# Decode attention beside an MLP on one core: from two-head to four-head groups, with hand-written waits

## The chip, the cores and the metric

The kernel runs on one core of one Trainium2 chip. A core has five engines that run their own instruction streams: TensorE (PE, matrix products into PSUM), VectorE (DVE), ScalarE (ACT), GpSimd (POOL) and SyncE (SP, which here only issues transfers). Sixteen DMA engines, called lanes below, move data between the chip's main memory (HBM) and the core's SBUF; SBUF and PSUM have 128 partitions. The metric is the device time of one execution in microseconds, lower is better; the median of the runs is given.

## The reference: what is computed

Four tokens (B = 4, one position each, D = 512) go through one block that adds two branches:

```
xn  = layernorm(x)
A   = attention(xn): q = xn @ wq, 32 heads of 128
      scores = q . k_cache * 128**-0.5        k_cache: [4, 32, 4096, 128]
      p = softmax(scores); o = p @ v_cache    v_cache: [4, 32, 4096, 128]
      return o @ wo
B   = mlp-mixer(xn): the shifts move along a sequence of length 1, so h @ w2 gets zeros
      x1 = xn;  return x1 + gelu(layernorm(x1) @ w3) @ w4
out = x + A + B
```

All data are 32-bit floats. The caches are 268 MB each and every byte of them is used once: 128 pairs of batch and head, each with 4096 keys and 4096 values of 128 elements. wq and wo are 8.4 MB each, w3 and w4 3.7 MB each. In all 561 MB are read.

## The kernel before

**Tiling.** Two heads are one pair, and there are 64 pairs. The keys of a pair are one contiguous stretch of 4 MiB. Partition p gets 64 consecutive rows of 128 elements, so one transfer is 128 rows of 32 KiB, eight for each lane, and partitions 0 to 63 hold the first head, 64 to 127 the second. Values lie in the same way. SBUF has six slots of 32 KiB a partition (`SLOTS = 6`), and keys, values and weights rotate through them.

**The loop over pairs** (`for i in range(NP + 1)`, L313) issues the transfers of the keys and values of pair i+1, works on the keys of pair i and finishes pair i-1:

- `products` (L205) multiplies the keys in place by the query on VectorE. The query has been spread to all partitions by a TensorE product (`queries`, L200) for four pairs at once and is read from PSUM. It is issued in two pieces of 2048 and 6144 elements.
- `row_sums` (L209) adds up each row of 128 products: 64 scores a partition.
- `max_begin` (L214, L216) takes each partition's maximum and turns the column of maxima into a row with a TensorE product; `weights` (L222 to L234) takes each head's maximum over that row, spreads its negative with another TensorE product, and has ScalarE compute exp(score - maximum) and its sums into `pw`.
- `values` (L244) contracts `pw` with the values: 16 TensorE products a pair (two records in the trace for each, 32-bit), four column groups side by side, into `PVS`.
- Every fourth pair `outputs` (L251 to L262) gathers and divides by the sums; every sixteenth `spread` (L265 to L268) writes a token's result to `X`.

**Around the loop.** `layernorm`, `transposed` and the query projection (L188) run while the first keys arrive. The MLP's upper half (L277 to L289) runs beside the first keys, its lower half (L307) near the end. wo arrives last in five pieces of falling size (`wo_load`, L346) and is multiplied by `X` in the same order (L358, L364, L369); the result is copied (L372) and stored (L374).

**What sets the order.** The source order above is each engine's order. The Tile framework puts the waits between the engines and between a buffer's last reader and its next transfer. All big transfers are issued from SP, in source order, in one queue; SP stops at a transfer whose slot is still in use. The loops are unrolled.

## Time and profile before

| what | us |
|---|---|
| median of 3 runs | 1317.51 |
| lowest and highest run | 1314.52, 1317.52 |
| span of the profiled execution, first to last instruction | 1312.6 |
| VectorE busy | 1161.9 (89%) |
| TensorE busy | 522.8 (40%) |
| ScalarE busy | 82.6 (6%) |
| all 16 lanes together, share of the span on the big queue | 99.4% |

The page gives the profiled execution its span, 1312.6 us, and no other time; the runs are 1.9 to 4.9 us above that span. The page's second part shows the span in 40 slices: one digit a slice is a busy share in tenths. The lines by engine name source line, engine, operation and tile, then how often they occur, the busy time in us and the mean of one in ns. A window row gives, for a stretch of the span, each engine's busy time with the number of instructions, the clock granted to TensorE as a share of full speed, the lanes' busy share and the GB/s they moved. In the timeline the first number of a row is the start in us, the second the duration.

### The profile page before, as it was taken

What the parts mean: (1) busy time and instruction counts of PE and PEld (TensorE: products, weight loads), DVE (VectorE), ACT (ScalarE), POOL (GpSimd) and SP (SyncE); (2) the same over time, 40 slices, a digit from 0 to 9 for tenths busy, and PEclk for the clock granted to TensorE, in tenths of its full rate; (3) what the DMA queues carried; (4) which work ended last, traced back from release to release, by engine and by line L of the source; (5) the groups of instructions that cost most, each with busy time, mean ns of one, the idle gap of its engine ahead of it and who ended that gap; (6) DMA issues with size and microseconds to landing.
All of it is one profiled execution on the core that took longest, in us unless ns stands there. A gap on an engine that the chain in (4) does not pass through costs nothing.

```text
span 1312.6 us, 6935 instructions
## 1 busy us (share of the span) xinstructions
PE 522.8 (40%) x2736; PEld 169.0 (13%) x2736; DVE 1161.9 (89%) x386; ACT 82.6 (6%) x349; POOL 15.4 (1%) x77
## 2 busy tenths in 40 slices
PE   5415334434424424434433433433443342443345
PEld 1101101111111101111110110111111110111111
DVE  2798999999999999989989999999999999999992
ACT  0100000000000000000000000000000000000000
POOL 0000000000000000000000000000000000000000
PEclk9666577566566666656656756756665756666768
DMA  9999999999999999999999999999999999999997
GB/s 404 434 432 430 431 430 432 431 431 432 433 431 431 430 432 430 430 432 432 432 431 431 432 431 431 431 431 432 432 431 431 432 431 431 431 431 431 433 431 314
DMA packets 19928, 561.46 MB, mean 428 GB/s; under 512 B 2220, under 2 KB 2228, under 8 KB 2488
## 3 DMA queue, kind: packets, MB, share of 16 engines
q1 hardware_dynamic: 19880, 561.00, 99.4%
q8 instruction: 22, 0.36, 0.1%
q14 instruction: 10, 0.08, 0.0%
q10 hardware_dynamic: 16, 0.01, 0.0%
HBM read 561.00 MB, written 0.01 MB: 427 GB/s over the span
## 4 chain that ended last, share of the span: by engine, by line
DMA 58%; DVE 33%; PE 6%; issue 2%; ACT 0%; SPq 0%; DVEq 0%
DMA k<-in_A_k_cache_dram 55%; DVE sc L209 19%; DVE k L205 13%; PE pv L244 4%; DMA wo<-in_A_wo_dram 3%; PE oz L254 1%; PE pm L216 0%; ACT os L251 0%; PE pn L224 0%; DVE gm L222 0%; DVE rm L214 0%; PE oz L257 0%; PE total L364 0%; PE total L369 0%; SPq L88 0%
## 5 line engine op out<-in xcount | busy, mean ns | idle before, releaser
L205 DVE TENSOR_TENSOR k<-k,qb 128x2048 f32<-128x2048 f32 (+1 forms) x128 | 560.0, 4415 | 58.1 <-DMA k<-in_A_k_cache_dram 57.9
L209 DVE TENSOR_REDUCE sc<-k 128x64 f32<-128x8192 f32 x64 | 555.5, 8679 | 4.9
L244 PE MATMUL pv<-v,pw 128*32 128x512 f32 x2048 | 371.2, 891 | 81.0 <-issue 79.8
L216 PE MATMUL pm<-ident,rm 128*1 128x128 f32 x128 | 37.4, 395 | 590.0 <-DVE rm L214 590.0
L244 PEld LDWEIGHTS pv<-v,pw 128*32 128x32 f32 x2048 | 92.9, 156 | 304.0 <-issue 302.7
L216 PEld LDWEIGHTS pm<-ident,rm 128*1 128x1 f32 x128 | 7.1, 80 | 635.8 <-issue 626.5
L226 ACT COPY nm<-pn 128x2 f32<-128x2 f32 x64 | 10.2, 160 | 1027.4 <-PE pn L224 1027.4
L222 DVE TENSOR_REDUCE gm<-pm 1x2 f32<-1x128 f32 x64 | 17.9, 279 | 50.0 <-PE pm L216 50.0
L224 PE MATMUL pn<-gm,ones 1*128 1x2 f32 x128 | 37.1, 357 | 24.3 <-DVE gm L222 24.3
L234 ACT ACTIVATE pw<-sc,nm 64x64 f32<-64x64 f32 x128 | 44.5, 347 | 6.0
L224 PEld LDWEIGHTS pn<-gm,ones 1*128 1x128 f32 x128 | 31.7, 305 | 56.2 <-DVE gm L222 53.4
L200 PE MATMUL qb<-q_sb,selb 64*128 64x512 f32 x32 | 19.9, 703 | 24.7 <-DVE k L205 24.0
L230 POOL MEMSET pw<- 128x128 f32 x64 | 13.0, 204 | 1229.9 <-PE pv L244 1229.9
L234 ACT ACTIVATION_READ_ACCUMULATOR pw<-sc,nm 64x1 f32 x128 | 23.6, 185 | 0.0
L254 PE MATMUL oz<-sel,os 128*128 128x8 f32 x128 | 16.9, 259 | 11.2 <-ACT os L251 11.2
L254 PEld LDWEIGHTS oz<-sel,os 128*128 128x128 f32 x128 | 15.5, 191 | 26.5 <-ACT os L251 26.5
L259 DVE RECIPROCAL rz<-oz 128x8 f32<-128x8 f32 x16 | 3.3, 205 | 15.3 <-PE oz L257 15.2
L214 DVE TENSOR_REDUCE rm<-sc 128x1 f32<-128x64 f32 x64 | 14.1, 220 | 1.7
L251 ACT COPY os<-pv 128x512 f32<-128x512 f32 x16 | 9.4, 585 | 94.8 <-PE pv L244 94.8
L267 PE MATMUL xt<-sel,lt 128*128 128x32 f32 x8 | 2.2, 365 | 29.3 <-DVE lt L265 29.3
L188 PE MATMUL pq<-wq,X 128*32 128x512 f32 x64 | 10.1, 792 | 9.2 <-DMA wq<-in_A_wq_dram 9.2
L372 DVE COPY q_sb<-total 64x256 f32<-64x256 f32 x1 | 0.4, 416 | 11.5 <-PE total L369 11.5
(77 smaller groups left out, 80.7 us busy)
## 6 DMA issues: line engine op xcount, KB each, us to landing
k<-in_A_k_cache_dram SPq DMA_DIRECT2D x64, 4096.0 KB, 40.7
v<-in_A_v_cache_dram SPq DMA_DIRECT2D x64, 4096.0 KB, 41.6
wq<-in_A_wq_dram SPq DMA_DIRECT2D x2, 4096.0 KB, 16.8
wo<-in_A_wo_dram SPq DMA_DIRECT2D x1, 4096.0 KB, 40.9
w<-in_B_w_dram SPq DMA_DIRECT2D x2, 1792.0 KB, 23.3
w<-in_B_w_dram SPq DMA_DIRECT2D x1, 3584.0 KB
wo<-in_A_wo_dram SPq DMA_DIRECT2D x1, 2048.0 KB, 35.9
wo<-in_A_wo_dram SPq DMA_DIRECT2D x1, 1024.0 KB
```

The source lines that it names most:

```text
L200: nc.tensor.matmul(QBC[z], selb[HALF * u:HALF * (u + 1), b], q_sb[HALF * u:HALF * (u + 1), n, :], start=True, stop=True)
L205: nc.vector.tensor_tensor(out=K[i][:, c0:c1, :], in0=K[i][:, c0:c1, :], in1=q, op=ALU.mult)
L209: nc.vector.reduce_sum(sc, K[i], axis=AX.X)
L214: nc.vector.reduce_max(rm, SC[i], axis=AX.X)
L216: nc.tensor.matmul(pm, rm, ident, start=True, stop=True)
L222: nc.vector.tensor_reduce(gm, ROWMAX[i].rearrange("o (e p) -> o e p", e=2), axis=AX.X, op=ALU.max, negate=True)
L224: nc.tensor.matmul(pn, ones[0:1, :], gm, start=True, stop=True)
L226: nc.scalar.copy(nm, pn)
L230: nc.gpsimd.memset(pw[:, :, 8 * r2:8 * r2 + 8], 0.0)
L234: nc.scalar.activation(o, sc[s, :].rearrange("p (g w) -> p g w", w=4), AF.Exp, bias=nm[s, e:e + 1], scale=1.0, accum_out=rs[s, r, e:e + 1])
L244: nc.tensor.matmul(pv[32 * t:32 * t + 32, :], pw[:, g, :], V[i][:, 4 * g:4 * g + 4, :], start=(r == 0 and g < 4), stop=(r == QUAD - 1 and ...
L254: nc.tensor.matmul(oz[:, 0, :], os[:, m, :], sel.rearrange("p (r m e) -> p m r e", m=4, e=2)[:, m], start=(m == 0), stop=(m == 3))
```

## The change

The whole kernel body is written anew; the sums it computes stay.

- Four heads are one group, 32 groups. One transfer is 8 MiB: 128 rows of 64 KiB. Partition p holds 128 rows of 128 elements, 32 partitions a head.
- SBUF holds three slots of 64 KiB a partition: keys rotate through two (S0, S1), values use one (S2). wq uses S2 first, w3 and w4 use S1, the small tensors of the start lie in S0. The last group's values go to S0 in three pieces, wo in five pieces to S2.
- The order of transfers on SP is wq (2), w3, w4, K0, K1, V0, K2, V1, K3 and so on. K0 waits for the queries (`d_Q`), K1 for the lower half of the MLP (`p_dn`), which now runs at the start; K(g+2) waits for the row sums of group g (`k_free`), V(g+1) for the contraction of group g (`v_free`).
- Each query is spread by VectorE: a copy that repeats its elements, then a transpose in blocks of 32 by 32 (`qx`, `qb`). Products and row sums are one instruction each, over 16384 elements, both inputs in SBUF. `contract` issues 32 TensorE products of 512 columns a group, `weights` four exponentials of 32 partitions each. The maxima are taken with a copy, a transpose and a reduction on VectorE. The TensorE products for spreading (L200, L224) and for turning maxima (L216) are gone, and POOL's clearing of `pw` (L230) too.
- The waits are written by hand. `own` makes VectorE wait for its own instruction; `take` is an instruction of its own that waits for a semaphore and takes the count back.
- The loops over groups are hardware loops (`Fori`) on TensorE, ScalarE and VectorE (two groups a turn on VectorE). SP's stream stays unrolled.
- The result is stored in four quarters instead of two halves.

The core of the diff, with the new stretches that the prediction speaks of:

```diff
-    R = 2 * S // P
-    NP = B * H // 2
-    kv = ctx.enter_context(tc.tile_pool(name="kv", bufs=SLOTS))
+    HG = 4
+    NG = B * H // HG
+    C = HG * S // P
+    G4 = C // 4
+    ROW = C * DH
+    slots = [sbuf(f"slot{i}", [P, ROW]) for i in range(3)]
...
+    def take(e, s, n=1):
+        e.wait_ge(s, n).then_inc(s, -n)
+    LAST = ((0, C // 2), (C // 2, 3 * C // 4), (3 * C // 4, C))
...
+        @block.sync
+        def _(e):
+            def load_k(g):
+                e.dma_start(KS[g % 2][:, :], group(kf, g)).then_inc(s_k[g % 2], 16)
...
+            e.wait_ge(d_Q, 1)
+            load_k(0)
+            e.wait_ge(p_dn, 1)
+            load_k(1)
+            for g in range(NG - 1):
+                if g > 0:
+                    take(e, v_free)
+                e.dma_start(S2[:, :], group(vf, g)).then_inc(s_v, 16)
+                if g + 2 < NG:
+                    take(e, k_free[g % 2])
+                    load_k(g + 2)
+            take(e, k_free[0])
...
+            take(e, v_free)
+            for n, (c0, c1) in enumerate(PIECES):
+                e.dma_start(wo_sb[:, c0:c1, :], wo_r[:, c0:c1, :]).then_inc(s_wo[n], 16)
...
+            with nc.Fori(0, NG - 1, 1, engines=[ET.PE]):
+                take(e, s_v, 16)
+                take(e, a_w)
+                contract(V3).then_inc(p_pv, 1)
+                outputs(v_free)
...
+            with nc.Fori(0, NG - 1, 1, engines=[ET.Activation]) as g:
+                weights()
+                e.drain().then_inc(a_sc, 1)
+                outputs(OS[:, bass.ds(g, 1), :])
...
+            with nc.Fori(0, NG, 2, engines=[ET.DVE]) as g:
+                for n in range(2):
+                    K = KS[n][:, :].rearrange("p (c d) -> p c d", c=C)
+                    own(e.tensor_copy(qx[:, :].rearrange("p (h r) -> p h r", h=4),
+                                      Q[:, bass.ds(g + n, 1), :].rearrange("p o h -> p (o h)").unsqueeze(2)
+                                      .to_broadcast([P, 4, 32])))
+                    own(e.transpose(qb[:, :], qx[:, :]))
+                    take(e, s_k[n], 16)
+                    own(e.tensor_tensor(out=K, in0=K, in1=qb[:, :].unsqueeze(1).to_broadcast([P, C, DH]), op=ALU.mult))
+                    take(e, a_sc)
+                    e.reduce_sum(sc[:, :], K, axis=AX.X).then_inc(d_self, 1)
+                    e.wait_ge(d_self, 1).then_inc(k_free[n], 1)
+                    own(e.reduce_max(st[:, 0:1], sc[:, :], axis=AX.X), 2)
+                    own(e.tensor_copy(mx[:, :], st[:, 0:1].to_broadcast([P, 32])))
+                    own(e.transpose(mt[:, :], mx[:, :]))
+                    e.tensor_reduce(st[:, 1:2], mt[:, :], axis=AX.X, op=ALU.max, negate=True).then_inc(d_m, 1)
```

In the new tail, chunks 0 to 23 of wo go to `y`, chunks 24 to 31 to `total` in four column groups of 128 columns each (two groups of 256 before).

## The prediction

> **What bounds the kernel now.** The first page is read from the top: busy shares, then the slices, then the queues.

> ```profile
> PE 522.8 (40%) x2736; PEld 169.0 (13%) x2736; DVE 1161.9 (89%) x386; ACT 82.6 (6%) x349; POOL 15.4 (1%) x77
> DMA  9999999999999999999999999999999999999997
> GB/s 404 434 432 430 431 430 432 431 431 432 433 431 431 430 432 430 430 432 432 432 431 431 432 431 431 431 431 432 432 431 431 432 431 431 431 431 431 433 431 314
> q1 hardware_dynamic: 19880, 561.00, 99.4%
> DMA k<-in_A_k_cache_dram 55%; DVE sc L209 19%; DVE k L205 13%; PE pv L244 4%; DMA wo<-in_A_wo_dram 3%; PE oz L254 1%; PE pm L216 0%; ACT os L251 0%; PE pn L224 0%; DVE gm L222 0%; DVE rm L214 0%; PE oz L257 0%; PE total L364 0%; PE total L369 0%; SPq L88 0%
> ```

> The lanes are busy in every slice but the last, at a steady 431 GB/s, and the big queue alone fills 99.4% of all lanes. VectorE is second with 89%. The chain of waits names VectorE for a third of the span, but that is an echo: it follows the keys' transfer back to the instruction that freed its slot, while the lanes went on with earlier transfers. 561.00 MB at 431 GB/s are 1301.6 us of the 1312.6 us span; 11 us are start and end. So the change can win only by moving the same bytes faster or by trimming the two ends, and it loses as soon as lanes run dry.

> ```profile
> SPq L95 <- DVE rm L214: 618.7, 60, 15.2
> SPq L99 <- PE pv L244: 516.6, 60, 9.8
> DVE k L205 <- DMA k<-in_A_k_cache_dram: 57.9, 53, 23.6
> ```

> These are the waits. SP waits for slots nearly all the time (618.7 and 516.6 us), yet the lanes don't idle, because transfers are queued ahead. VectorE waits for keys only 57.9 us in all, 23.6 of them for the first: it has little slack.

> **What one packet costs.** The queue view for two stretches, a steady one (100 to 1250 us) and the end, where wo's small pieces arrive (1300 to 1308 us): first all packets, then the big queue's packets, MB and share of 16 lanes.

> ```profile
> DMA packets 17039, 495.91 MB, mean 431 GB/s; under 512 B 1889, under 2 KB 1889, under 8 KB 1889
> q1 hardware_dynamic: 17011, 495.53, 100.2%
> DMA packets 389, 1.85 MB, mean 231 GB/s; under 512 B 53, under 2 KB 53, under 8 KB 296
> q1 hardware_dynamic: 388, 1.83, 55.6%
> q8 instruction: 1, 0.02, 0.9%
> ```

> The packets under 512 B are the transfers' completions; I charge them to the data. Steady: 17011 - 1889 = 15122 packets of 32 KiB took 100.2% x 16 x 1150 us = 18437 us, 1219 ns each. End: 388 - 53 = 335 packets of 5463 B on average took 55.6% x 16 x 8 us = 71.2 us, 212 ns each. The line through both is 0.0369 ns a byte plus 11 ns a packet. Keys and values are 16384 packets before and 8448 after (63 transfers of 128 and the last values in three pieces): 7936 x 11 ns / 16 lanes = **5.5 us less**. Bounds: nothing if a 64 KiB row costs what two of 32 KiB do (no row shows so large a packet), 6.4 us if the fixed part is 13 ns. I take the line. [...]

> **VectorE for four heads.** Groups by form, busy us and mean ns of one:

> ```profile
> L209 DVE TENSOR_REDUCE sc<-k 128x64 f32<-128x8192 f32 x64 | 555.5, 8679 | 4.9
> L205 DVE TENSOR_TENSOR k<-k,qb 128x6144 f32<-128x6144 f32 x64 | 418.9, 6545 | 0.0
> L205 DVE TENSOR_TENSOR k<-k,qb 128x2048 f32<-128x2048 f32 x64 | 146.2, 2285 | 58.1 <-DMA k<-in_A_k_cache_dram 57.9
> L222 DVE TENSOR_REDUCE gm<-pm 1x2 f32<-1x128 f32 x64 | 17.9, 279 | 50.0 <-PE pm L216 50.0
> L214 DVE TENSOR_REDUCE rm<-sc 128x1 f32<-128x64 f32 x64 | 14.1, 220 | 1.7
> L288 DVE STREAM_TRANSPOSE w<-w 128x448 f32<-128x448 f32 x1 | 0.6, 645 | 0.0
> L289 DVE COPY gT<-w 128x56 f32<-128x56 f32 x1 | 0.2, 191 | 0.0
> ```

> Before, two pairs cost 2 x (8.679 + 6.545 + 2.285 + 0.279 + 0.220) = 36.0 us. The two products give 1.04 ns an element plus 155 ns, the two reductions L209 and L214 the same slope. So 16384 elements cost 17.19 and 17.20 us. The small ones, moved along that slope: copies of 128 and 32 elements 0.27 and 0.17 us (from L289), transposes of 128 and 32 0.31 and 0.21 (from L288), reductions of 128 and 32 0.29 and 0.19 (from L214). Sum 35.8 us: larger instructions save what the transposes cost. On top come ten `take` and `own` waits and half a loop turn. A wait that is an instruction of its own stands before L234 on ScalarE:

> ```profile
> 1249.78 0.16 ACT L226 COPY nm<-pn 128x2 f32<-128x2 f32 x1 [18.30 <-PE pn L224]
> 1250.02 0.35 ACT L234 ACTIVATE pw<-sc,nm 64x64 f32<-64x64 f32 x1
> 1251.01 6.27 PE L244 MATMUL pv<-v,pw 128*32 128x512 f32 x32 [1.27 <-issue]
> ```

> The gap there is 0.08 us; I take 0.1 us a wait and 0.3 us for the loop, T = **37.1 us** a group. The lanes need 16.78 MB / 431 GB/s = 38.9 us, less 0.18 for the packets: 38.7. VectorE stays hidden, with 1.6 us to spare a group (38.9 - 36.0 = 2.9 before). The dropped TensorE, ScalarE and POOL steps (L200, L216, L224, L226, L230) lay beside the lanes and are worth nothing; so do the larger exponentials.

> **Do three slots keep the lanes fed?** Take group g in the steady state, its keys' last byte at 0. V(g-1), K(g+1), V(g) follow, 19.4 us each. K(g+2) must be issued before V(g) ends at 58; it waits for row sums that end near 35. V(g+1) must be issued before K(g+2) ends, 19.4 us after V(g) landed; it waits for one contraction of 32 products. A pair's 16 take 6.27 us in the row above, so 12.5 us, and everything queued behind that `take` on SP is one transfer. Adding 1 us from issue to first byte, some 5 us are left. Cost nothing; without that cover, each us over costs 30 us.

> The tightest point is the start:

> ```profile
> 0.74 0.38 SPq L103 DMA_DIRECT2D w<-in_B_w_dram  x1
> 27.77 5.20 PE L188 MATMUL pq<-wq,X 128*32 128x512 f32 x32 [4.78 <-DMA wq<-in_A_wq_dram]
> 32.19 0.60 ACT L191 ACTIVATE q_sb<-pq 128x512 f32<-128x512 f32 x1 [21.13 <-PE pq L188]
> 37.53 8.75 DVE L205 TENSOR_TENSOR k<-k,qb 128x2048 f32<-128x2048 f32 x2 [23.57 <-DMA k<-in_A_k_cache_dram]
> ```

> wq's second half was there at 27.8 behind 1.8 MB of w3, which now come later: 23.5. Product 5.2, scaling twice 0.6, transpose of 1024 elements 1.2 and a copy 0.3: K0 is issued near 31, while w3 and w4 keep the lanes busy until 40. K1 waits for the MLP's lower half and must be queued before K0 ends at 59.5: that leaves w3's reader 28 us from w3's landing near 32 for a dozen short steps (L288 and L289 above are two) and 60 records of products at the rate of L188, some 15 us in all. VectorE starts K0 at 60, its row sums end at 60 + 34.4 + 0.3 = 94.7, and K2 must be issued before V0 ends at 98: 3 us to spare, less on lanes that run ahead. I take 0; bounds 0 and +2. Each later group gains 1.6 us of slack. The start has two more branch and semaphore steps on SP ahead of its first transfer (at 0.74 above): +0.4, bounds 0 and +1.

> **The end.** Lanes, and the chain of the last pair:

> ```profile
> 1300.00:1302.00 2.00, 2.00 (x24) 0.45 (x19) 0.00 (x0) 0.00 (x0) 0.00 (x0) 1.00 0.94 389
> 1302.00:1304.00 2.00, 1.49 (x16) 0.22 (x12) 0.00 (x0) 0.00 (x0) 0.00 (x0) 1.00 0.70 289
> 1304.00:1306.00 2.00, 1.45 (x16) 0.30 (x10) 0.00 (x0) 0.58 (x1) 0.00 (x0) 1.00 0.50 203
> 1306.00:1308.00 2.00, 2.00 (x22) 0.89 (x18) 0.00 (x0) 0.00 (x0) 0.00 (x0) 1.00 0.12 42
> ```

> ```profile
> 1288.87 0.35 ACT L234 ACTIVATE pw<-sc,nm 64x64 f32<-64x64 f32 x1
> 1289.81 5.64 PE L244 MATMUL pv<-v,pw 128*32 128x512 f32 x32 [1.22 <-ACT pw L234]
> 1298.79 0.21 ACT L268 COPY X<-xt 128x32 f32<-128x32 f32 x1 [2.67 <-PE xt L267]
> 1299.05 3.62 PE L358 MATMUL y<-wo,X 128*4 128x512 f32 x32 [0.30 <-ACT X L268]
> 1303.18 1.90 PE L358 MATMUL y<-wo,X 128*4 128x512 f32 x16 [0.51 <-DMA wo<-in_A_wo_dram]
> 1305.63 1.90 PE L364 MATMUL total<-wo,X 128*4 128x256 f32 x16 [0.55 <-DMA wo<-in_A_wo_dram]
> 1309.73 0.42 DVE L372 COPY q_sb<-total 64x256 f32<-64x256 f32 x1 [11.51 <-PE total L369]
> ```

> The lanes' share falls from 0.94 to 0.12 over 8 us: they end at different times, and the slowest sets the end; 3.5 us a lane are lost on average. Something delays single lanes; each 16 KiB instruction packet (0.9% of 16 lanes over 8 us, 1.2 us on one lane) does. With loops there are fewer of those: -1.2 us, bounds 0 and -3.

> After K31 lands, V30, V31 and wo follow, 25.2 MB or 58.4 us. Keys 34.4, maxima and waits 2.0, four exponentials 2.1, contraction 2 x 5.64, and from there to X 3.6 us as in the rows (1295.45 to 1299.0): X is there 53.4 us after K31, 5 us before wo's last byte. The 24 first chunks (3.62 + 1.90) end 0.5 us behind it, the other eight some 2 to 3 us later. Before, the products ended at 1309.7, 2 us after the last bytes: **+0.7 us**, bounds -1 and +3.

> **Sum:** -5.5 + 0.4 + 0 - 1.2 + 0.7 = -5.6 us: a span of 1307.0. The span before is 4.9 us under the median of the runs, 1317.5; with that distance kept the time is 1311.9 us.

> **Rivals.**
> A. The large packet wins nothing (two 32 KiB packets' cost inside one). For it: no row shows 64 KiB. Against: the line through 5 and 32 KiB. Time 1311.9 + 5.5 = 1317.4, no change. Chance 0.14.
> B. VectorE becomes the bound, slower. All of VectorE's groups follow one another, from K0's landing at 60 to the last maxima, then 2.1 + 11.3 + 3.6 + 5.5 + 2.5 + 0.4 + 2.5 (store) = 27.9: span 60 + 32 T + 27.9. It passes 1307.0 at T = 38.1, that is if a wait costs 0.2 us instead of 0.1. At 0.28 T is 38.9, the time 60 + 1245 + 27.9 + 4.9 = 1338. For it: 320 new waits. Against: the gap of 0.08 us. Chance 0.11.
> C. A loop's jump back stalls VectorE while its instructions come from memory again: one or two packets of 1.2 us plus 1 us of latency each, at two packets 4.4 us for two groups, T = 39.3: 60 + 1258 + 27.9 + 4.9 = 1351. No row shows a loop here. [...] Chance 0.07.
> D. The single value slot starves the lanes: contraction, landing and issue exceed 19.4 us. It takes 5 us more than the rows give; one us over is 30 us: about 1342. Chance 0.06.

> **How the numbers follow.** The forecast keeps 0.62, with its own range 1306 to 1316. About 0.3% (4 us) is what a measurement of this kernel can tell from no change; the forecast lies 5.6 us below, so of its 0.62 I count 0.54 as faster and 0.08 as the same. A gives 0.01 faster, 0.11 same, 0.02 slower; B, C and D 0.24 slower. Faster 0.55, same 0.19, slower 0.26. The forecast and A hold 0.76; the range 1305 to 1324 takes them in, with A's 1317.4 plus its bounds of +2 and +3, and the mildest part of B and D.

> **What would show it.** Right: about 9600 data packets on the big queue, 433 GB/s in the middle slices; products and row sums at 17.2 us; VectorE waiting 1 to 2 us for every K; no slice with a lane share under 1 before the last. Wrong: 431 GB/s again (A); VectorE with no wait for keys and lanes under 1.00 throughout (B, C: gaps of 0.2 us at each wait, or of us at every second group); SP waiting for the contraction while lanes idle (D); a dip near 98 us (start). Two things would break it unseen: a product slower than 1.04 ns an element with both inputs in SBUF, or 64 KiB rows that slow the memory itself.

## The result, and the profile after

The changed kernel takes 1313.37 us (median of 20 runs, 1311.78 to 1315.70), the kernel before 1317.34 us (median of 20, 1313.42 to 1318.03). The ratio is 0.998, with a 95% interval of 0.9972 to 0.9987: faster, by 1.7 to 3.7 us, where 5.6 were forecast. The medians lie 4.0 us apart because 12 of the 20 times of before lie in an upper group, 1316.8 to 1318.0, which the last experiments take up. Measured once more (below) it is 0.999, interval 0.9982 to 0.9999. The profiled execution took 1314.01 us with a span of 1312.2.

The page of the changed kernel answers to the page lines of before:

```profile
PE 370.9 (28%) x2652; PEld 134.9 (10%) x2652; DVE 1162.1 (89%) x297; ACT 98.5 (8%) x333; POOL 1.9 (0%) x10
DMA  9999999999999999999999999999999999999995
GB/s 404 440 434 420 442 436 428 441 424 443 422 443 434 430 439 426 439 426 443 420 443 438 426 439 428 439 424 443 430 434 436 430 439 426 443 420 443 436 422 235
q8 instruction: 3, 0.05, 0.0%
```

No slice of the lanes is under 9 but the last, so three slots do feed them, and the start has no dip. VectorE is still at 89%. The last slice is emptier than before (235 GB/s against 314): the lanes are done earlier, and the kernel ends no earlier. The queue view for 100 to 1250 us gives the rate:

```profile
DMA packets 8553, 498.56 MB, mean 434 GB/s; under 512 B 944, under 2 KB 944, under 8 KB 944
q1 hardware_dynamic: 8551, 498.54, 100.2%
```

7607 packets of 64 KiB took 100.2% x 16 x 1150 us, 2424 ns each; two of 32 KiB took 2 x 1219 = 2438. So 14 ns are saved on each 64 KiB, 7 us over the caches; the shares are printed to 0.1%, so the 14 is good to some 2 ns. VectorE's groups by form, with the mean of one in ns and the idle time before them:

```profile
L363 DVE TENSOR_TENSOR slot<-slot,qb 128x16384 f32<-128x16384 f32 x32 | 551.2, 17225 | 49.4 <-DVEq L70 49.4
L365 DVE TENSOR_REDUCE sc<-slot 128x128 f32<-128x16384 f32 x32 | 551.0, 17220 | 8.2 <-DVEq L70 8.2
L358 DVE COPY qx<-Q 128x128 f32 x32 | 7.2, 226 | 4.6 <-issue 4.6
```

Products and row sums come out at the 17.2 us forecast. The wait for keys (L70 is `take`) is 49.4 us, 16.8 of them for the first. The 4.6 us ahead of L358 are the hardware loop's jumps back: 0.31 us for each of the 15 between its 16 turns.

The end, in the timeline of the changed kernel (start, duration, instruction, idle time before it):

```profile
1241.58 17.22 DVE L363 TENSOR_TENSOR slot<-slot,qb 128x16384 f32<-128x16384 f32 x1 [1.79 <-DVEq L70]
1277.55 0.18 DVE L370 TENSOR_REDUCE st<-mt 128x1 f32<-128x32 f32 x1 [0.15 <-DVEq L70]
1279.81 0.20 ACT L282 ACTIVATION_READ_ACCUMULATOR pw<-sc,st 32x1 f32 x1
1281.36 0.61 PE L168 MATMUL ps<-sel,lt 128*128 128x32 f32 x2 [8.93 <-PEq L70]
1284.19 0.60 PE L168 MATMUL ps<-sel,lt 128*128 128x32 f32 x2 [0.81 <-PEq L70]
1284.72 9.57 PE L168 MATMUL ps<-slot,pw 128*32 128x512 f32 x64
1298.54 0.21 ACT L294 COPY X<-ps 128x32 f32<-128x32 f32 x1 [2.04 <-ACTq L70]
1298.80 8.49 PE L168 MATMUL ps<-slot,X 128*4 128x512 f32 x80 [0.39 <-ACT X L294]
1306.49 0.58 ACT L307 COPY os<-ps 128x512 f32<-128x512 f32 x1 [7.75 <-PE ps L168]
1308.50 0.29 DVE L382 COPY res<-ps 128x128 f32<-128x128 f32 x1 [10.84 <-PE ps L168]
```

The exponentials end at 1280.01, where the forecast has them (38.5 us behind K31). But the contraction starts at 1284.72: the first three tokens' spreads stand ahead of it in TensorE's stream, and each goes through VectorE, TensorE and ScalarE in turn. `X` is ready at 1298.75, and the 24 first chunks of wo then take 7.7 us, to 1306.49, instead of 5.5. The windows say why:

```profile
1296.00:1298.00 2.00, 0.40 (x3) 0.35 (x4) 0.84 (x3) 0.17 (x1) 0.00 (x0) 0.66 0.91 366
1298.00:1300.00 2.00, 1.61 (x10) 0.54 (x14) 0.00 (x0) 0.21 (x1) 0.00 (x0) 0.50 0.14 53
1300.00:1302.00 2.00, 2.00 (x12) 0.30 (x8) 0.00 (x0) 0.00 (x0) 0.00 (x0) 0.50 0.04 8
1302.00:1304.00 2.00, 2.00 (x16) 0.40 (x12) 0.00 (x0) 0.00 (x0) 0.00 (x0) 0.64 0.00 0
```

The granted clock is at 0.50, against 1.00 in the rows of before, and the lanes are all but empty from 1300 on. This end is a chain of instructions; nothing in it waits for a byte.

### The profile page after: what moved, and what is told of

It is laid out like the page before. It is cut to its first block, busy times and chain, and to the rows that moved or that the text cites. A ratio compares the mean times of both kernels' runs of the same rounds, so it can differ in the third digit from the quotient of the medians.

```text
span 1312.2 us, 6970 instructions
## 1 busy us (share of the span) xinstructions
PE 370.9 (28%) x2652; PEld 134.9 (10%) x2652; DVE 1162.1 (89%) x297; ACT 98.5 (8%) x333; POOL 1.9 (0%) x10
## 3 DMA queue, kind: packets, MB, share of 16 engines
q1 hardware_dynamic: 10816, 561.00, 98.9%
HBM read 561.00 MB, written 0.01 MB: 428 GB/s over the span
## 5 line engine op out<-in xcount | busy, mean ns | idle before, releaser
L363 DVE TENSOR_TENSOR slot<-slot,qb 128x16384 f32<-128x16384 f32 x32 | 551.2, 17225 | 49.4 <-DVEq L70 49.4
L365 DVE TENSOR_REDUCE sc<-slot 128x128 f32<-128x16384 f32 x32 | 551.0, 17220 | 8.2 <-DVEq L70 8.2
L168 PE MATMUL ps<-slot,pw 128*32 128x512 f32 x2048 | 290.9, 732 | 883.0 <-PEq L70 883.0
L168 PEld LDWEIGHTS ps<-slot,pw 128*32 128x32 f32 x2048 | 79.7, 132 | 1068.8 <-issue 1068.7
L282 ACT ACTIVATE pw<-sc,st 32x128 f32<-32x128 f32 x128 | 67.3, 526 | 349.5 <-ACTq L70 348.1
L288 ACT COPY os<-ps 128x512 f32<-128x512 f32 x32 | 18.7, 585 | 765.1 <-ACTq L70 765.1
L168 PE MATMUL ps<-sel,os 128*128 128x4 f32 x256 | 32.8, 252 | 18.1 <-PEq L70 18.1
L168 PEld LDWEIGHTS ps<-sel,os 128*128 128x128 f32 x256 | 31.0, 191 | 19.9 <-issue 19.9
L282 ACT ACTIVATION_READ_ACCUMULATOR pw<-sc,st 32x1 f32 x128 | 26.2, 205 | 0.0
L375 DVE RECIPROCAL rec<-OS 128x32 f32<-128x32 f32 x4 | 1.4, 349 | 14.8 <-ACT OS L290 12.5
L168 PE MATMUL ps<-rs,ones 128*128 128x4 f32 x64 | 12.3, 263 | 0.0
L358 DVE COPY qx<-Q 128x128 f32 x32 | 7.2, 226 | 4.6 <-issue 4.6
L342 DVE STREAM_TRANSPOSE slot<-slot 128x1024 f32<-128x1024 f32 x1 | 1.2, 1245 | 11.1 <-ACT slot L269 11.1
L369 DVE STREAM_TRANSPOSE mt<-mx 128x32 f32<-128x32 f32 x32 | 6.8, 211 | 4.7
L368 DVE COPY mx<-st 128x32 f32<-128x32 f32 x32 | 5.8, 181 | 4.7
## 6 DMA issues: line engine op xcount, KB each, us to landing
slot<-in_A_wo_dram SPq DMA_DIRECT2D x1, 2048.0 KB, 23.6
```

The costliest lines, as they stand in the source:

```text
L168: return e.matmul(o, l, r, start=start, stop=stop)
L282: i = e.activation(o, sc[r, :].rearrange("p (g w) -> p g w", w=4), AF.Exp, bias=st[r, 1:2], scale=1.0, accum_out=rs[r, h:h + 1])
L288: e.copy(os[:, :, :], pv[:, :].rearrange("p (m d) -> p m d", m=4)).then_inc(a_os, 1)
L358: own(e.tensor_copy(qx[:, :].rearrange("p (h r) -> p h r", h=4), Q[:, bass.ds(g + n, 1), :].rearrange("p o h -> p (o h)").unsqueeze(2) .to ...
L363: own(e.tensor_tensor(out=K, in0=K, in1=qb[:, :].unsqueeze(1).to_broadcast([P, C, DH]), op=ALU.mult))
L365: e.reduce_sum(sc[:, :], K, axis=AX.X).then_inc(d_self, 1)
```

## The experiments

The theory that they test: the lanes deliver as forecast, and the gain is lost at the end, in the spreads ahead of the contraction and in the granted clock. The rivals: the lanes gained less than they seem to, VectorE is the bound, or wo's last bytes hold the end. From the last maxima's end to the span's end the changed kernel takes 1312.2 - 1277.7 = 34.5 us; the experiments on the end are read by this distance too, since the last keys land up to 2.6 us apart from one execution to the next, with the same transfers. The runs come from several chips: each ratio is to the kernel before on the same chip, and a difference in us between two runs can hold a difference between chips.

**The changed kernel again.** No edit.

> The changed kernel once more, as the base for the edits beside it. Median near 1313.4 us (1311.8 to 1315.7), the span 1.8 us under the time in each execution, the same tail: last bytes of wo near 1299.5, end of the products near 1308.4.

Median 1314.71 us (12 runs, 1311.91 to 1315.43), beside 1315.13 for before. That is 1.3 us above the median that was expected; the medians of before move by up to 2.9 us from one measurement to the next (1314.41 to 1317.34). It is the other measure for the changed kernel below.

**Spreads inside the contraction.**

```diff
-            for b in range(B - 1):
-                spread(b)
             take(e, a_w)
-            for n, (c0, c1) in enumerate(LAST):
-                e.wait_ge(s_vl[n], 16)
+            for n, (c0, c1) in enumerate(((0, 32), (32, 64), (64, 96), (96, 128))):
+                e.wait_ge(s_vl[max(n - 1, 0)], 16)
                 i = contract(VL, c0 // 4, c1 // 4)
+                if n < B - 1:
+                    spread(n)
```

> The three spreads of tokens 0 to 2 stand between four pieces of the last contraction instead of ahead of it. Theory 1 (the end is set by the compute chain that starts when the last keys land; the spreads held the last contraction back from 1280.1 to 1284.7, 4.6 us): the contraction starts right behind the last exponentials, three spreads of 0.6 us lie in it, the result comes 2.5 to 3.5 us earlier, about 1310.4 us. Rival (the transfers or the store still set the end): within 0.5 us of the changed kernel. Rival (the contraction starts earlier but at a lower clock and loses it again): 0 to 1 us.

1310.38 us (1309.40 to 1312.61), ratio to before 0.9956 (0.9944 to 0.9969). Its timeline:

```profile
1279.80 0.19 DVE L370 TENSOR_REDUCE st<-mt 128x1 f32<-128x32 f32 x1
1282.06 0.20 ACT L282 ACTIVATION_READ_ACCUMULATOR pw<-sc,st 32x1 f32 x1
1282.41 3.40 PE L168 MATMUL ps<-slot,pw 128*32 128x512 f32 x16 [7.62 <-PEq L70]
1296.89 8.97 PE L168 MATMUL ps<-slot,X 128*4 128x512 f32 x80 [0.39 <-ACT X L294]
```

The contraction follows the exponentials within 0.2 us. From the maxima to the end it is 30.8 us instead of 34.5, and the time falls by 3.0 to 4.3 us against the two medians of the changed kernel. wo's products stay slow (8.97 us).

**Unused products in TensorE's pause.**

```diff
                 i = mm(oz[:, HG:2 * HG], ones[:, :], rs[:, :], True, True)
+                if done is None:
+                    for t in range(4):
+                        mm(pb[32 * t:32 * t + 32, :], sel[:, :], VL[:, 4 * t:4 * t + 4, :], True, True)
...
                 i.then_inc(p_oz, 1)
+            for t in range(8):
+                mm(pb[32 * (t % 4):32 * (t % 4) + 32, :], sel[:, :], VL[:, 4 * t:4 * t + 4, :], True, True)
             spread(B - 1)
```

> Twelve unused TensorE products of 512 columns are put into TensorE's idle time between the last contraction and the first product with wo. Theory 1 (the 24 first wo products took 7.7 us instead of 5.5 because the granted clock had fallen to 0.50 after 4.6 us of little work): the clock stays at 1.00 and the wo products need 5.5 to 6 us, so 1.5 to 2.2 us less, about 1311.5 us. Rival (they are slow because the pieces of wo land late or the operands come from elsewhere): clock up, time the same within 0.5 us.

1311.89 us (1310.78 to 1312.86), ratio 0.9967 (0.9954 to 0.998). One window row and wo's products:

```profile
1300.00:1302.00 2.00, 2.00 (x20) 0.49 (x24) 0.00 (x0) 0.00 (x0) 0.00 (x0) 1.00 0.08 28
```

```profile
1299.95 6.21 PE L168 MATMUL ps<-slot,X 128*4 128x512 f32 x80 [0.39 <-ACT X L299]
```

The clock stays at 1.00 and the same 80 records take 6.21 us instead of 8.49, while the lanes are as empty. So the clock made them slow, not wo's landing.

**Both.** The two edits above together.

> Both edits of the end at once: the three earlier tokens' spreads lie between four pieces of the last contraction, and twelve unused products keep TensorE busy between that contraction and wo's products. Theory 1 (the end is one chain from the last group's maxima, and nothing the lanes do after that matters): the changed kernel needs 34.5 us from the end of the last maxima to the end of the span, the moved spreads alone 30.8, the unused products alone 32.2; the two gains add, 28.5 us here, so with maxima at 1278 to 1280 a span of 1306.5 to 1308.5 and a time of 1308.3 to 1310.3. Theory 2 (the last bytes of wo, near 1299.5 to 1301.7, hold the end once X is there before them): X comes near 1296.5, the 24 first chunks wait for pieces, at least 30 us from maxima to end, time 1310 to 1312, as with the moved spreads alone. Theory 3 (the clock falls by how long TensorE has worked, not by idling just before): the wo products stay near 8.5 us.

1309.14 us (1308.45 to 1309.95), ratio 0.9951 (0.9937 to 0.9966). wo's products are one stretch without a wait:

```profile
1277.41 0.19 DVE L375 TENSOR_REDUCE st<-mt 128x1 f32<-128x32 f32 x1 [0.15 <-DVEq L70]
1280.03 3.64 PE L168 MATMUL ps<-slot,pw 128*32 128x512 f32 x16 [7.86 <-PEq L70]
1284.16 2.80 PE L168 MATMUL ps<-slot,pw 128*32 128x512 f32 x16
1287.23 1.92 PE L168 MATMUL ps<-slot,pw 128*32 128x512 f32 x16
1296.23 6.21 PE L168 MATMUL ps<-slot,X 128*4 128x512 f32 x80 [0.39 <-ACT X L299]
```

The distance is 29.8 us, not 28.5: the contraction's first half still runs at half pace (3.64 and 2.80 us against 1.92), which the sum left out. The time is in the first theory's range.

**A clock raised for the contraction too**, by twelve unused products ahead of it:

```diff
+            e.wait_ge(s_vl[0], 16)
+            for t in range(12):
+                mm(pb[32 * (t % 4):32 * (t % 4) + 32, :], sel[:, :], VL[:, 4 * t:4 * t + 4, :], True, True)
             take(e, a_w)
```

> Moved spreads and unused products as in the run with both, and twelve more unused products of 512 columns ahead of the last contraction, whose first half ran at a granted clock of 0.50 there (16 records 3.64 us and 2.80 us, against 1.92 for the later ones). Theory 1 (the end is still one chain): the contraction is 1.5 to 2.5 us shorter and the time falls with it, from 1309.1 to 1306.6 to 1307.8. Theory 2 (the last bytes of wo, at 1299.5 to 1301.7, now hold the end): wo's products wait for their pieces and the time falls by less than 1 us, 1308.2 to 1309.1. Rival (the unused products delay the contraction themselves): 1309.5 to 1311.

1309.66 us (1308.24 to 1310.92): nothing gained, and none of the three expectations tested:

```profile
1272.75 2.78 PE L168 MATMUL ps<-slot,sel 128*32 128x512 f32 x24
1280.87 3.64 PE L168 MATMUL ps<-slot,pw 128*32 128x512 f32 x16 [5.34 <-PEq L70]
```

The products took only 2.78 us, and 5.34 us without work followed, after which the contraction is as slow as without them. The time lies in the rival's range, but the contraction was not held up: it starts 2.4 us behind the maxima, as in the run with both edits. With `range(24)`, over the same sixteen blocks:

> As in the run with twelve unused products ahead of the last contraction, but twenty-four, because those twelve took only 2.78 us and left TensorE 5.3 us without work, after which the contraction's first half ran at 0.50 again. Now they reach to about 2.5 us before the contraction. Theory 1 (the end is one chain and a pause shorter than 3 us leaves the clock): the contraction is 1.5 to 2.5 us shorter, the time 1306.6 to 1308. Theory 2 (the last bytes of wo now hold the end): less than 1 us gained, 1308.2 to 1309.5, wo's products in more than one stretch. Rival (the clock falls all the same): 1309 to 1310.5.

1307.47 us (1306.40 to 1308.91), ratio to before 0.9939 (0.9925 to 0.9952), the fastest version here.

```profile
1277.50 0.19 DVE L378 TENSOR_REDUCE st<-mt 128x1 f32<-128x32 f32 x1 [0.15 <-DVEq L70]
1280.11 1.92 PE L168 MATMUL ps<-slot,pw 128*32 128x512 f32 x16 [1.88 <-PEq L70]
1293.49 6.21 PE L168 MATMUL ps<-slot,X 128*4 128x512 f32 x80 [0.39 <-ACT X L302]
```

After a pause of 1.88 us the contraction runs at full pace from its first record, and the distance is 26.9 us. wo's products are still one stretch: even now its bytes don't hold the end.

**Packets of 32 KiB again**, with the slots and waits of the changed kernel:

```diff
+            def halves(slot, rows, s):
+                for c in range(2):
+                    c = slice(c * ROW // 2, (c + 1) * ROW // 2)
+                    e.dma_start(slot[:, c], rows[:, c]).then_inc(s, 16)
...
-                e.dma_start(KS[g % 2][:, :], group(kf, g)).then_inc(s_k[g % 2], 16)
+                halves(KS[g % 2], group(kf, g), s_k[g % 2])
...
-                e.dma_start(S2[:, :], group(vf, g)).then_inc(s_v, 16)
+                halves(S2, group(vf, g), s_v)
...
-                take(e, s_v, 16)
+                take(e, s_v, 32)
...
-                    take(e, s_k[n], 16)
+                    take(e, s_k[n], 32)
```

> Each transfer of keys or values is cut into two of 4 MiB, 128 rows of 32 KiB each, into the same slots with the same waits; the last values stay as they are. Theory (a packet has a fixed cost, 64 KiB packets took 2424 ns against 2 x 1219 ns): 8064 packets more, 6 to 7 us more on each lane, the last keys land that much later, and since the end hangs on them 1319.5 to 1320.5 us; middle slices at 431 GB/s. Rival (the gain of the stream came from the fewer instruction packets or the order of the transfers): under 1315 us and 433 GB/s.

1318.69 us (1316.88 to 1319.54), ratio to before 1.0018 (1.0009 to 1.0027): 4.0 and 5.3 us over the two medians of the changed kernel. The last group's product:

```profile
1245.88 17.22 DVE L368 TENSOR_TENSOR slot<-slot,qb 128x16384 f32<-128x16384 f32 x1 [1.94 <-DVEq L70]
```

K31 comes 4.3 us later than in the changed kernel's profile, and everything behind it too; it is 2.0 us later than in the latest of the profiles above (1243.83, with the moved spreads). The time is 0.8 us under the theory's range. The larger packet is worth what was forecast, within 1.5 us.

**TensorE's loop written out.**

```diff
-            with nc.Fori(0, NG - 1, 1, engines=[ET.PE]):
+            for _ in range(NG - 1):
```

> TensorE's hardware loop is written out, 31 times the same 37 products; everything else as in the changed kernel. It separates the loops' part of the gain from the packets' part. Theory (instruction fetches slow single lanes): some 20 instruction packets of 16 KiB instead of 3, each 1.2 us on one lane; the last bytes of the lanes in a transfer lie up to 5 us apart instead of 1.9, the last keys land 1 to 3 us later, and as the end is a chain from them the time rises by 1 to 3 us, to 1314.5 to 1317. Rival (the fetches cost nothing, and all of the earlier last byte comes from the packets): spread and time as in the changed kernel, 1312 to 1315. Second rival (the loop itself costs TensorE time that counts): faster than the changed kernel, under 1312.

1317.12 us (1315.57 to 1318.69), ratio to before 1.0013 (1.0004 to 1.0023): 2.4 and 3.7 us over the changed kernel. The page's queue, the windows at the end, and the last product:

```profile
q8 instruction: 21, 0.34, 0.1%
```

```profile
1296.00:1298.00 2.00, 1.42 (x14) 0.58 (x5) 0.00 (x0) 0.59 (x1) 0.00 (x0) 1.00 0.87 358
1298.00:1300.00 2.00, 0.78 (x7) 0.69 (x7) 0.61 (x3) 0.17 (x1) 0.00 (x0) 0.75 0.61 252
1300.00:1302.00 2.00, 1.24 (x6) 0.61 (x10) 0.23 (x1) 0.21 (x1) 0.00 (x0) 0.50 0.33 132
1302.00:1304.00 2.00, 2.00 (x16) 0.41 (x12) 0.00 (x0) 0.00 (x0) 0.00 (x0) 0.50 0.02 9
```

```profile
1244.33 17.23 DVE L363 TENSOR_TENSOR slot<-slot,qb 128x16384 f32<-128x16384 f32 x1 [1.88 <-DVEq L70]
```

With 18 instruction packets more the lanes' share falls over 6 us, 0.87, 0.61, 0.33, 0.02, where the changed kernel has 0.91, 0.14, 0.04, and the last keys come 2.75 us later than in its profile. That is only 0.5 us later than in the latest of the others (1243.83), so the medians carry the result, not this row. At 1.2 us each (0.9% of 16 lanes over 8 us, in the row of before for 1300 to 1308 us), 18 packets spread over 16 lanes would cost 18 x 1.2 / 16 = 1.4 us. Why more is lost is not shown: the theory has single lanes delayed, and no view here shows single lanes.

**More work on VectorE.** The edit is a maximum over 32 rows of 128 elements, and so over 4096 elements, twice what the expectation says:

```diff
+                    own(e.reduce_max(st[:, 2:3], K[:, 0:32, :], axis=AX.XY))
                     take(e, a_sc)
```

> One more VectorE instruction for each group, a maximum over 2048 elements ahead of the row sums, with its own wait: about 2.15 + 0.2 us by the slope of the row sums (17.22 us for 16384). Its result is not used. It tests how near VectorE is to being the bound. Theory (37.05 us of work a group against 38.7 of the lanes, 1.6 us spare): 39.4 us a group, VectorE never waits for keys after the first, the last maxima end at 60.7 + 32 x 39.4 = 1321.5, the span at 1356, time 1355 to 1361, and the lanes' share falls below 1. Rival 1 (VectorE is covered with room to spare): only the last group is later, 1315 to 1317. Rival 2 (VectorE is the bound already, its waits being an artefact of the records): 32 x 2.35 = 75 us more, 1389.

1435.51 us (two runs). The timeline has two products two groups apart, the added instruction, and the last maxima:

```profile
646.95 17.23 DVE L363 TENSOR_TENSOR slot<-slot,qb 128x16384 f32<-128x16384 f32 x1 [0.26 <-DVEq L70]
664.32 4.42 DVE L364 TENSOR_REDUCE st<-slot 128x1 f32<-128x4096 f32 x1
...
730.66 17.23 DVE L363 TENSOR_TENSOR slot<-slot,qb 128x16384 f32<-128x16384 f32 x1 [0.26 <-DVEq L70]
...
1398.86 0.19 DVE L371 TENSOR_REDUCE st<-mt 128x1 f32<-128x32 f32 x1
```

VectorE no longer waits for keys, and two groups take 83.7 us, 41.85 each. Less 4.42 and 0.14 for the added instruction that is 37.3 us of work a group, against 37.1 forecast and 38.7 of the lanes: 1.4 us to spare. With the instruction's true size the first theory gives 60.7 + 32 x 41.6 + 34.5 = 1426; the span is 1433.6, since a group takes 0.2 us more. Had VectorE been the bound already (rival 2), 32 x 4.56 = 146 us would have been added; the runs show 121 to 122. So the form of the sum holds, and rival B needs 1.4 us of further work a group.

**The kernel before, for its spans.** No edit.

> The kernel before, for its spans: its times fall in two groups, 1313.4 to 1315.1 and 1316.4 to 1318.0, and only one span, 1312.6, is known. Theory 1 (what lies around the span is the same 1.8 us as in the changed kernel): every run's time is 1.7 to 1.9 us over its span, so the groups have spans near 1312.3 and 1315.3, and the difference arises on the chip within the span. Theory 2 (the distance varies): spans all near 1312.6, and time minus span falls in two groups near 1.8 and 4.9 us, as the prediction took it.

Time minus span is 1.79 to 1.92 us in all 11 runs: eight spans lie in 1311.9 to 1313.2, three in 1315.1 to 1315.8. The distance doesn't vary, the execution does. The profiled one has the longer span, and the end differs from the profile in the prediction:

```profile
1298.00:1300.00 2.00, 1.08 (x7) 0.90 (x6) 0.67 (x3) 0.00 (x0) 0.00 (x0) 0.66 0.94 393
1300.00:1302.00 2.00, 1.70 (x11) 0.27 (x14) 0.00 (x0) 0.21 (x1) 0.00 (x0) 0.50 0.95 394
...
1304.00:1306.00 2.00, 2.00 (x16) 0.38 (x12) 0.00 (x0) 0.00 (x0) 0.00 (x0) 0.64 0.41 167
```

The clock is at 0.50 from 1298.6 to 1305.4 here, during wo's products, and at 1.00 there.

**The kernel before with its pause filled.** Twelve unused products behind the last outputs, in the source:

```diff
+        def unused(n):
+            if z == NQ - 1:
+                pd = psum.tile([P, P], F32, tag="b", name=f"pd{n}")
+                for _ in range(n):
+                    nc.tensor.matmul(pd, ident, ones, start=True, stop=True)
+        unused(4)
...
         nc.tensor.matmul(oz[:, 1, :], ones, RS[z % 2], start=True, stop=True)
+        unused(8)
```

> The kernel before, with twelve unused products of 128 columns in TensorE's pause between the last contraction and wo's products. It tests why the kernel before has two groups of times, 1313.4 to 1315.3 and 1316.4 to 1318.0. The two profiles of it differ at the end: with a span of 1312.6 the granted clock is 1.00 throughout wo's products, with a span of 1315.1 it is 0.50 from 1299 to 1305 and 48 records take 7.85 us. Theory (the pause of 3 to 4 us is about as long as the stretches by which the clock is granted, so that it depends on chance whether the clock falls in it): with the pause filled the clock stays at 1.00, all times lie in 1313.3 to 1315.5, none above 1316. Rival (the groups come from somewhere else, the clock goes with them by accident): a third to a half of the times remain in 1316.4 to 1318.0.

1317.33 us (1315.31 to 1318.30), and no test of the question: as the products depend on nothing, they stand ahead of the last contraction in the trace, which they delayed, and the pause stayed (3.8 us from the contraction's end to wo's products). That 10 of its 11 times lie at 1316.90 or above, where before has them in part only, is left open.

```profile
1289.32 4.74 PE L257 MATMUL pd<-ones,ident 128*128 128x128 f32 x24
1301.45 7.94 PE L365 MATMUL y<-wo,X 128*4 128x512 f32 x48 [0.30 <-ACT X L275]
```

Six products that read the copied sums can't run ahead of the contraction:

```diff
         nc.tensor.matmul(oz[:, 1, :], ones, RS[z % 2], start=True, stop=True)
+        if z == NQ - 1:
+            pd = psum.tile([P, P], F32, tag="b", name="pd")
+            for n in range(6):
+                nc.tensor.matmul(pd, os[:, n % 4, :], ident, start=True, stop=True)
```

> The kernel before once more with unused products, six of 128 columns, which now read the copied sums and so cannot run ahead of the last contraction: they stand between the last outputs' products and the last token's spread, where TensorE pauses. They may hold that spread up by 0.4 us. Theory (the two groups of times come from the granted clock during wo's products, which falls or not by chance in this pause): with it filled the clock stays at 1.00, all times lie in 1313.7 to 1315.7, none above 1316. Rival (the groups have another origin): a third to a half of the times lie in 1316.8 to 1318.4.

1314.53 us, and all 11 runs lie in 1314.19 to 1315.70, while 5 of 15 runs of the kernel before on the same chip lie in 1316.85 to 1317.76.

```profile
1299.29 1.58 PE L261 MATMUL pd<-ident,os 128*128 128x128 f32 x12
1301.32 5.33 PE L362 MATMUL y<-wo,X 128*4 128x512 f32 x48 [0.30 <-ACT X L272]
```

The 48 records take 5.33 us, not 7.94. If a third of the runs fell into the upper group by chance, eleven without one would have a probability of about 1%. So the upper group of before's times comes from the granted clock in its last pause. With the clock kept up during wo's products in both kernels, the change is worth some 1314.53 - 1311.89 = 2.6 us, an estimate from two chips.

## Why the prediction was right in its direction and wrong in its size

- **Packets, -5.5 us: right.** 14 ns a 64 KiB by the packets' own time, 7 us over the lanes, a little over the upper bound of 6.4; 4.0 to 5.3 us of the end by the run with 32 KiB. Rival A falls.
- **VectorE at 37.1 us, hidden: right** (37.3; a wait leaves gaps of about 0.15 us, not 0.1: the page has 4.7 us ahead of the 32 copies of L368). Rival B did not come, and neither did C: a jump back costs 0.31 us, and the changed kernel's page has 3 instruction packets on q8 and 3 on q14 (0.05 and 0.02 MB) beside 15 jumps back, so VectorE's loop was not fetched anew each turn.
- **Slots and start: right.** No dip at 98 us, no starving for values (D); the first product starts at 60.33 to 60.74 in the profiles, forecast 60. The first transfer is issued at 0.96 us instead of 0.74, so the +0.4 for the start was about +0.2.
- **The lanes' spread, -1.2: right in kind, too small.** TensorE's loop alone is worth 2.4 to 3.7 us, inside the upper bound of 3 or a little over it.
- **The end, +0.7: this step failed.** From K31's product to the end of the span the forecast has 64.3 us (53.4 to `X`, 5.5, 2.5, 0.4 and 2.5), the trace 1312.2 - 1241.6 = 70.6. The terms: the spreads ahead of the contraction +4.6, not costed at all, though `spread` stands before `take(e, a_w)` in the new source; the contraction -1.7 (9.57 against 11.28); from it to `X` +0.9; wo's first 24 chunks at half the clock +2.2; the rest of wo -0.5; the store, 3.4 us behind the last copy against 2.5, +0.9. These make 6.4. The two large ones have a run each: moving the spreads takes 3.7 us off the distance from the maxima to the end, keeping the clock takes off 2.3 (1311.1 - 1278.9 = 32.2). The contraction's -1.7 is the clock again: the forecast doubled a row that ran mostly at 0.50 (the first 4.1 of its 5.64 us), and here the clock rose halfway (at 1289.8, 5.1 us into 9.57). No run isolates the +0.9 before `X` and the +0.9 of the store; their causes stay open.
- **"X is there 5 us before wo's last byte" fell with it.** It was the cover of that term. `X` came at 1298.75, the lanes were empty by 1300, and from there on every further us of the chain was paid in full.
- **The baseline.** 4.9 us between span and median was kept as a fixed distance. It is 1.7 to 1.9 in the runs of both kernels; the profile shown is an execution of some 1314.4 us with the clock at 1.00 at its end, and the median of 1317.5 was one of the others. Against its own span the sum said -5.6, and the trace says 1312.2 - 1312.6 = -0.4: what the lanes gained by ending some 8 us earlier went into the end. In the medians the loss at the end looks smaller, since 12 of before's 20 runs lie in the group that paid for the clock too. That the forecast of 1311.9 came within 1.5 us of the measured 1313.4 is in part luck: the span of 1307.0 was 4.6 us too short against the runs' median span of 1311.6, and the distance of 4.9 us was 3.1 too long.

## What to carry to other kernels

When a change speeds up the transfers of a kernel bound by them, cost the tail behind the last transfer instruction by instruction, in the order of each engine's new stream: this one gave nearly all of its gain back there, most of it through three small products ahead of the one that mattered and through a lower clock. Look at the granted clock in the windows of the last microseconds, and give TensorE something to do in pauses like those here (3.8 us and more lowered the clock, 1.88 us did not) ahead of products on the critical path, with an operand that keeps it in its place. Compare a span with the time of its own execution, and ask whether the profiled one belongs to the same group of runs as the median.
